# An attention and feed-forward kernel: the early batches' leftover scores beside the second visit, and one output block a half later

## The chip, the cores and the metric

The kernel runs on one core of a Trainium2 chip. The metric is the device time of one execution in microseconds. Kernel before: median 320.42 us of 13 runs (319.06 to 323.31).

## What is computed

Attention with a relative position bias over 8 batches, 8 heads, 576 positions and 64 dimensions per head, then a feed-forward layer that takes the largest of three products. In short:

```
scores = q @ k.T / 8 + bias_table[bucket(|i - j|)]     # per batch and head, 576 x 576
attn   = softmax(scores) @ v
x      = attn, heads side by side                       # 4608 tokens x 512
h      = max(x @ w1, x @ w2, x @ w3)                    # 4608 x 768
out    = h @ w_out                                      # 4608 x 512, float32
```

The bucket depends on the distance alone and is constant beyond a limit, so the bias is applied as a factor after the exponential, in a band near the diagonal only; elsewhere it is a constant that cancels in the softmax.

## The kernel before

**Tiles.** 576 positions are four tiles of 128 and a leftover of 64. Heads go in pairs (hp 0 to 3). A pair's exponentials lie in e4 (four key tiles, two heads, 512 queries) and in el, which takes the leftovers: first the leftover 64 keys of both heads against all 576 queries ("left keys", score tile sct, lines 573 to 581), then the leftover 64 queries against the four key tiles ("left queries", score tile scq, 547 to 551 and 589 to 594).

**The loop over pairs** (813 to 894; batches 1 to 7, four pairs each; batch 0 has loops of its own ahead of it). A pair is worked in two halves, each of which begins with a visit (554 to 571): for 256 queries, two score tiles sc of eight matmuls in all, each with a 1024-wide exponential on ScalarE. Between the visits stand the attention products of the pair before (attend, 604 to 652), the leftover scores, the band multiplications on VectorE (times_band, 529 to 536), and matmuls of the feed-forward layer of tokens that are done.

**attend** is kept back in a list, late, two entries for a pair: half 0 has 18 matmuls, half 1 has 27, since it also takes the leftover queries. Each accumulates in one bank of ps_a. Its quotients (638 to 651) are a reciprocal and a multiplication on VectorE; for the last pair of a batch they also issue transposing DMAs on SyncE's queue that put the result in xT, which the feed-forward layer reads.

**PSUM.** Three pools with two buffers each, handed out in turn: ps_s (two banks each: sc, sct, scq of left_queries, and tp, the transposes of batch 1's queries and keys), ps_a (one bank: attention sums, and scq in the new way), ps_f (one bank: feed-forward products, outputs, the x transposes).

**Two ways for a pair.** In line 818, together is true for batches 3 to 7 and for (2, 1) to (2, 3). There the left queries are scored in the second visit, ahead of its sc tiles, in two ps_a banks, with two 256-wide exponentials (556 to 559); both attention halves of the pair before run in the first half, the second one right after the left keys (844 to 847); and the second half's fill runs with idle_sums set, so that the feed-forward layer's first products use ps_a (339). For batch 1 and (2, 0), attention half 1 follows the second visit (860 to 863), and the left queries are scored inside the second fill, in a ps_s buffer, with one 512-wide exponential (880 to 881).

**Order.** All matmuls and transposes (93 to 97), VectorE's operations and most DMA issues are kept in program order; the exponentials and some ScalarE copies are not pinned. In batch 1, second_transposes (507 to 527, called in line 865) stands behind the second visit; it makes the next pair's qT and kT by ten transposes into one ps_s buffer and copies on VectorE and ScalarE.

**The fill** (439 to 451). The feed-forward layer is cut in portions with a weight that counts 128x512 matmuls (two 128x256 ones count as one). fill(rate, hooks) takes portions, at least one, until the next would pass the rate, and calls its hooks just before the last groups of these. Rate is 8 in batch 1 and (2, 0), else 13 (819). The portions that fall to the pairs concerned, in units of a 128x512 matmul, first half + second half: (1, 0) and (1, 1) 4 + 8, (1, 2), (1, 3) and (2, 0) 8 + 4, (2, 1) 12 + 6. The 12 are two output blocks of six matmuls (output, 362 to 393), the 6 a third one.

**Loads.** load_qk(3) in line 874 is gated by the quotients of attend(1, 3, 1); it is issued on GpSimd's queue. load_v(2) in line 871 stands ahead of it there.

Of the kernel before, what the change touches and what calls it, by code (L numbers as in the profile page):

```python
# [39 lines left out]
def kernel(  # L40
# [21 lines left out]
    QM = 2 * QS  # L62
# [28 lines left out]
    inorder = tc.keep_in_program_order  # L91

    def mm(*args, **kw):
        inorder(nc.tensor.matmul(*args, **kw))  # L94
# [322 lines left out]
    pending, rest, stores, deferred, idle_sums = [], [], [], [], []  # L417

    def store_outputs():

        while stores:
            stores.pop(0)()
# [7 lines left out]
    def early():  # L430

        if pending and None in pending[0][1]:
            n, fns = pending[0]
            i = fns.index(None)
            for fn in fns[:i]:
                fn()
            pending[0] = (n, fns[i + 1 :])

    def fill(target, *hooks):

        groups, spent, hooks = [], 0, list(hooks)
        while pending and (not groups or spent + pending[0][0] <= target):
            n, fns = pending.pop(0)
            spent += n
            groups += [fn for fn in fns if fn]
        for j, group in enumerate(groups):
            while hooks and (j == len(groups) - 1 or j > 0 and len(hooks) > len(groups) - 1 - j):
                hooks.pop(0)()
            group()
        for hook in hooks:  # L450
            hook()


    def transposes(b):

        made = qk_tiles()
        qk.append(made)

        def one(j, t):
            n = P if t < KT or j else S - KT * P  # L460
            src = batch[b][j][:, t].rearrange("p h d -> p (h d)") if t < KT else (
                (qtail, ktail)[j][b % 2][0:n].rearrange("p h c -> p (h c)")
            )
            turned_qk[b, j, t] = inorder(nc.sync.dma_start_transpose(out=made[j][:, :, P * t : P * t + n], in_=src))  # L464

        for t in range(KT + 1):
            one(0, t)
            one(1, t)
            yield
# [59 lines left out]
    def times_band(hp, e4, t, lo, hi, put=lambda x: x):  # L529
        lo, hi = max(lo, P * t - P), min(hi, P * t + 2 * P)  # L530
        if lo < hi:
            c0, c1 = BAND - (hi - P * t + P), BAND - (lo - P * t + P)
            put(nc.vector.tensor_tensor(  # L533
                out=e4[:, t, :, lo:hi], in0=e4[:, t, :, lo:hi],
                in1=hank[:, 2 * hp : 2 * hp + 2, c0:c1][:, :, ::-1], op=ALU.mult,
            ))

    def exp(out_, in_):
        nc.scalar.activation(out=out_, in_=in_, func=ACTF.Exp, scale=inv_sqrt_d)  # L539

    def put_left_queries(el, banks):

        eq = el[:, S:].rearrange("p (t h q) -> p t h q", t=KT, h=2)
        for par, bank in enumerate(banks):
            exp(eq[:, :, par, :], bank.rearrange("p (t q) -> p t q", t=KT))

    def turn_left_queries(qT, kT, banks):

        for t in range(KT):
            for par, bank in enumerate(banks):  # L550
                r = slice(64 * par, 64 * par + 64)
                mm(bank[:, 64 * t : 64 * t + 64], lhsT=kT[r, P * t : P * t + P], rhs=qT[r, QM:S])

    def visit(qT, kT, e4, c, mid=None, el=None):

        if el is not None:
            banks = [ps_a.tile([P, KT * 64], F32, tag="a", name="scq") for _ in range(2)]
            turn_left_queries(qT, kT, banks)
            put_left_queries(el, banks)
        for tt in range(0, KT, 2):  # L560
            sc = ps_s.tile([P, 2, 2, QS], F32, tag="sc", name="sc")
            for t in range(2):
                for par in range(2):
                    r = slice(64 * par, 64 * par + 64)
                    mm(
                        sc[:, par, t, :], lhsT=kT[r, P * (tt + t) : P * (tt + t) + P],
                        rhs=qT[r, c * QS : c * QS + QS],
                    )
            exp(e4[:, tt : tt + 2, :, c * QS : c * QS + QS].rearrange("p t h q -> p h t q"), sc[:])
            if tt == 0 and mid:  # L570
                mid()
# [17 lines left out]
    def left_queries(hp, qT, kT, el):  # L589

        sc = ps_s.tile([P, 2, CH], F32, tag="sc", name="scq")
        turn_left_queries(qT, kT, [sc[:, par, 0 : KT * 64] for par in range(2)])
        eq = el[:, S:].rearrange("p (t h q) -> p h t q", t=KT, h=2)
        exp(eq, sc[:, :, 0 : KT * 64].rearrange("p h (t q) -> p h t q", t=KT))
# [70 lines left out]
    def x_tile():  # L665
        return xs.tile([P, KT + 1, d_model], BF16, tag="x_sb", name="x_sb")
# [3 lines left out]
    def next_late():  # L670
        return late.pop(0)() if late else (lambda: None)

    def e_tiles():
        return (
            ep.tile([P, KT, 2, QM], BF16, tag="e4", name="e4"),
            ep.tile([P, S + KT * P], BF16, tag="el", name="el"),
        )
# [49 lines left out]
    for hp in range(HP):  # L727
        qT, kT = (x[:, hp, :] for x in qk[0])
        e4, el = e_tiles()
# [28 lines left out]
    for hp in range(HP):  # L758
        qT, kT = (x[:, hp, :] for x in qk[0])
        e4, el = e_tiles()  # L760
# [11 lines left out]
        def keys():  # L772
            left_keys(hp, qT, kT, el, QS, S)
# [7 lines left out]
        quotients = next_late()  # L781
# [5 lines left out]
        if hp < 2:  # L787
# [5 lines left out]
            quotients = next_late()  # L793
# [19 lines left out]
    for b, hp in [(b, hp) for b in range(1, B) for hp in range(HP)]:  # L813
        if hp == 0:
            x_sb[b] = x_tile()
        qT, kT = (x[:, hp, :] for x in qk[b])
        e4, el = e_tiles()
        together = b > 1 and (b, hp) != (2, 0)
        rate = 8 if b == 1 or (b, hp) == (2, 0) else 13

        visit(qT, kT, e4, 0)
        store_outputs()
        if b == 1:
            if hp == 0:
                crossbar = transposes(2)
            next(crossbar, None)
        elif hp and b + 1 < B:
            if hp == 1:  # L830
                crossbar = transposes(b + 1)
            next(crossbar)
        early()
        if turned:
            turned.pop(0)()
        quotients = next_late()
        times_band(hp, e4, 0, 0, QS, inorder)
        quotients()
        if b == 1 and hp + 1 < HP:
            spread_packed(hp + 1, nc.vector)  # L840
        if (b, hp) == (1, 1):
            add_ffn(QS, QS)

        def keys():
            left_keys(hp, qT, kT, el, 0, S)
            if together:
                next_late()()

        fill(rate, keys, *([lambda: None] if together else []))
        times_bandt(hp, el)  # L850


        visit(qT, kT, e4, 1, el=el if together else None)
        store_outputs()
        if b == 1 or hp in (1, 2) and b + 1 < B:
            next(crossbar, None)
        early()
        if turned:
            turned.pop(0)()
        if not together:  # L860
            quotients = next_late()
            times_band(hp, e4, 1, 0, QM, inorder)
            quotients()
        if b == 1 and hp + 1 < HP:
            second_transposes(qk[1], hp + 1)
        if hp == 1 and b > 1:
            add_ffn((b - 1) * CH, CH)
        if hp == (2, 2, 0)[min(b, 3) - 1] and b + 1 < B:
            if b == 1:
                load_last_weights(turned_qk[2, 1, 1])  # L870
            load_v(b + 1, 0, H, turned_qk[b + 1, 1, KT - 1] if b < 3 else None)
        if (b, hp) == (2, 0):
            batch[3] = load_tiles()
            load_qk(3, divided[1, HP - 1, 1])
        if hp == 2 and 1 < b < B - 2:
            batch[b + 2] = load_tiles()
            load_qk(b + 2, turned_qk[b + 1, 1, KT - 1])

        def queries():
            if not together:  # L880
                left_queries(hp, qT, kT, el)
            times_band(hp, e4, 3, 0, QM, inorder)

        def bands_2():
            for t in range(1 if together else 2, 3):
                times_band(hp, e4, t, 0, QM, inorder)

        if together:
            idle_sums.append(hp)
        fill(rate, bands_2, queries)  # L890
        idle_sums.clear()
        times_band_left(hp, el)
        for half in range(2):
            late.append(lambda b=b, hp=hp, e4=e4, el=el, half=half: attend(b, hp, e4, el, half))
# [44 lines left out]
```

## Time and profile before

| | |
|---|---|
| median of 13 runs | 320.42 us |
| the profiled execution: time, span | 321.07 us, 319.3 us |
| TensorE busy | 306.3 us (96%) |
| VectorE busy | 213.4 us (67%) |
| ScalarE busy | 201.1 us (63%) |
| GpSimd busy | 108.3 us (34%) |
| 1024-wide exponential (sc) | 128 of 1030 ns |
| 576-wide exponential (sct) | 28 of 655 ns |
| 512-wide exponential (scq, old way) | 9 of 598 ns |
| 256-wide exponential (scq, new way) | 46 of 381 ns |
| granted TensorE clock | full, but for 18.2 to 25.0 us of the span, where it is half |

How to read the profile: times are microseconds unless marked ns; a row gives the source line, the engine, the operation, output and input by the program's names, the shape and the count. PE is TensorE's matmuls, PEld its weight loads, DVE VectorE, ACT ScalarE, POOL GpSimd, SP SyncE. Matmuls overlap in the pipeline, so what a group of them costs is read from the start of one group to the start of the next and not from their lengths. Line 94 is the helper that issues every matmul, so the groups are told apart by their tiles.

### The profile page before, as it was taken

The numbers are of one execution on the slowest core, as the hardware profiler recorded it, in microseconds if no ns is written. First come the engines' busy times: TensorE is split into PE (matmuls) and PEld (weight loads), VectorE is DVE, ScalarE is ACT, GpSimd is POOL, SyncE is SP. The second block draws the span as 40 slices with busy tenths as digits, with TensorE's granted clock in tenths as the row PEclk, the third lists the DMA queues.
The fourth block names the chain that finished last, engine by engine and source line by source line (L and its number), as shares of the span: only waits on it lengthen the run. The fifth ranks groups of instructions, "written<-read, shape, count | busy, mean of one in ns | idle before, by whom it ended". The sixth has DMA issues, their size and how long they took to land.

```text
span 319.3 us, 8238 instructions
## 1 busy us (share of the span) xinstructions
PE 306.3 (96%) x3328; PEld 172.0 (54%) x3328; DVE 213.4 (67%) x535; ACT 201.1 (63%) x297; POOL 108.3 (34%) x143
## 2 busy tenths in 40 slices
PE   7768999999999999999999999999999999999995
PEld 2346777775555555555555555555555555444442
DVE  6387778786667766666677767777667675554552
ACT  4958998896777667766777677667776751121221
POOL 8938741348049530952087019600000000000000
PEclk9969999999999999999999999999999999999999
DMA  9999999999999999999999999994042103301103
GB/s 165 192 198 199 182 144 134 142 109 140 193 152 151 130 199 163 85 131 196 175 83 146 161 204 119 154 223 95 2 77 99 36 2 74 133 0 71 62 0 131
DMA packets 163878, 40.34 MB, mean 126 GB/s; under 512 B 153720, under 2 KB 159360, under 8 KB 163840
## 3 DMA queue, kind: packets, MB, share of 16 engines
q0 software_dynamic: 103776, 16.66, 79.1%
q1 hardware_dynamic: 58304, 22.69, 39.6%
q10 hardware_dynamic: 1760, 0.47, 0.7%
q8 instruction: 26, 0.43, 0.6%
q14 instruction: 12, 0.10, 0.1%
HBM read 35.39 MB, written 9.45 MB: 140 GB/s over the span
## 4 chain that ended last, share of the span: by engine, by line
PE 70%; DMA 3%; SPq 2%; ACT 1%; DVE 0%; issue 0%; DVEq 0%
PE ps L94 37%; PE pso L94 13%; PE a L94 11%; PE sc L94 6%; DMA kT<-ktail 2%; SPq L464 2%; PE sct L94 2%; PE scq L94 1%; DMA out_dram<-osb 1%; ACT e L539 0%; DVE m L354 0%; ACT osb L388 0%; ACT osb L107 0%; SPq L389 0%; DVE el L585 0%
## 5 line engine op out<-in xcount | busy, mean ns | idle before, releaser
L94 PE MATMUL ps<-xT,w_bf 128*128 128x512 bf16 (+1 forms) x720 | 152.2, 358 | 0.0
L539 ACT ACTIVATE e<-sc 128x1024 bf16<-128x1024 f32 x128 | 124.3, 1030 | 20.5 <-PE sc L94 18.1
L94 PEld LDWEIGHTS <-w_bf 128*128 128x128 bf16 x720 | 65.3, 98 | 62.7 <-issue 5.0
L533 DVE TENSOR_TENSOR e<-e,hank 128x512 bf16<-128x512 bf16 (+2 forms) x136 | 59.0, 469 | 12.0 <-ACT e L539 9.9
L345 ACT ACTIVATE m<-ps 128x512 bf16<-128x512 f32 x48 | 29.2, 608 | 51.9 <-PE ps L94 51.9
L354 DVE TENSOR_TENSOR m<-ps,m 128x512 bf16<-128x512 f32 x48 | 33.1, 689 | 34.2 <-PE ps L94 34.0
L94 PE MATMUL pso<-wo_bf,hT 128*128 128x512 bf16 (+2 forms) x222 | 50.3, 373 | 0.0
L94 PEld LDWEIGHTS <-kT 64*128 64x128 bf16 (+1 forms) x832 | 29.8, 95 | 37.2 <-issue 24.0
L94 PE MATMUL a<-vx,e 128*128 128x65 bf16 x1024 | 46.4, 195 | 0.0
L94 PE MATMUL sc<-qT,kT 64*128 64x256 bf16 x512 | 41.0, 273 | 2.9 <-ACT e L539 1.3
L360 DVE TENSOR_TENSOR hT<-ps,m 128x512 bf16<-128x512 f32 x48 | 33.0, 688 | 15.9 <-PE ps L94 14.5
L94 PEld LDWEIGHTS <-e 128*128 128x128 bf16 x1024 | 42.1, 99 | 0.8
L139 POOL DMA_DIRECT2D vx<-in_v_dram x32 | 28.3, 905 | 30.2 <-DMA kT<-k_sb 13.5
L94 PE MATMUL a<-vt,el 128*128 128x130 bf16 x160 | 36.0, 225 | 1.2 <-DMA vt<-in_v_dram 1.2
L167 POOL DMA_DIRECT2D q_sb<-in_q_dram x24 | 22.0, 918 | 43.9 <-DMA kT<-k_sb 12.9
L110 DVE COPY osb<-pso 128x512 f32<-128x512 f32 (+1 forms) x33 | 22.6, 686 | 18.0 <-PE pso L94 14.7
L641 DVE TENSOR_TENSOR x_sb<-a,rd 128x256 bf16<-128x256 f32 (+1 forms) x64 | 31.4, 491 | 2.2
L539 ACT ACTIVATE el<-scq 128x256 bf16<-128x256 f32 (+1 forms) x55 | 20.5, 416 | 19.5 <-PE scq L94 19.4
L94 PEld LDWEIGHTS <-hT 128*128 128x128 bf16 x222 | 20.1, 97 | 22.4 <-issue 1.5
L94 PEld LDWEIGHTS <-el 128*128 128x128 bf16 x416 | 24.3, 97 | 10.4 <-issue 5.5
L539 ACT ACTIVATE el<-sct 128x576 bf16<-128x576 f32 (+2 forms) x36 | 21.7, 606 | 6.6 <-PE sct L94 5.3
L167 POOL DMA_DIRECT2D k_sb<-in_k_dram x24 | 22.1, 919 | 1.2 <-DMA w_bf<-in_moe_w_dram 1.2
(71 smaller groups left out, 168.2 us busy)
## 6 DMA issues: line engine op xcount, KB each, us to landing
out_dram<-osb SPq DMA_DIRECT2D x35, 256.0 KB, 3.1
vx<-in_v_dram POOLq DMA_DIRECT2D x32, 128.0 KB, 8.3
q_sb<-in_q_dram POOLq DMA_DIRECT2D x26, 128.0 KB, 6.0
k_sb<-in_k_dram POOLq DMA_DIRECT2D x24, 128.0 KB, 6.8
w_bf<-in_moe_w_dram POOLq DMA_DIRECT2D x3, 768.0 KB, 10.5
xT<-in_k_dram SPq DMA_DIRECT2D x6, 128.0 KB, 4.5
hank<-w_dr SPq DMA_DIRECT2D x2, 384.0 KB, 6.4
wo_bf<-in_moe_w_out_dram POOLq DMA_DIRECT2D x1, 768.0 KB, 8.3
```

The source lines that it names most:

```text
L94: inorder(nc.tensor.matmul(*args, **kw))
L110: return inorder(nc.vector.tensor_copy(out_, in_))
L139: in_turn(b, nc.gpsimd.dma_start(out=dst[:, t, h0:h1, :], in_=x[:, t, h0:h1, :])) for t in range(t0, t1)
L167: loads.append(in_turn(b, nc.gpsimd.dma_start(out=dst[:, t], in_=main_part(src, b)[:, t])))
L345: nc.scalar.activation(out=st[fb]["m0"][:], in_=ps0, func=ACTF.Copy)
L354: inorder(nc.vector.tensor_tensor(out=m[:], in0=ps1, in1=st[fb]["m0"][:], op=ALU.max))
L360: inorder(nc.vector.tensor_tensor(out=block(fb), in0=ps2, in1=other, op=ALU.max))
L464: turned_qk[b, j, t] = inorder(nc.sync.dma_start_transpose(out=made[j][:, :, P * t : P * t + n], in_=src))
L533: put(nc.vector.tensor_tensor(out=e4[:, t, :, lo:hi], in0=e4[:, t, :, lo:hi], in1=hank[:, 2 * hp : 2 * hp + 2, c0:c1][:, :, ::-1], op=ALU. ...
L539: nc.scalar.activation(out=out_, in_=in_, func=ACTF.Exp, scale=inv_sqrt_d)
L641: divided[b, hp, half] = inorder(nc.vector.tensor_tensor(out=x_sb[b][:, 2 * half : 2 * half + n, P * hp : P * hp + P].rearrange("p t (h d) ...
```

## The change

All pairs from batch 1 on are done the one way. For batch 1 and (2, 0) this means: attention half 1 of the pair before moves from behind the second visit into the first fill, right after the left keys; the left queries move from the second fill into the second visit, ahead of its score tiles, from one ps_s buffer to two ps_a banks, with two exponentials instead of one; band 1 moves into the second fill; idle_sums is set there. The second hook of the first fill does nothing and moves the left keys a group ahead where there are three groups or more. In (2, 1) the first fill gets rate 8 instead of 13, so that one of its two output blocks goes to the second half.

```diff
-        together = b > 1 and (b, hp) != (2, 0)
         rate = 8 if b == 1 or (b, hp) == (2, 0) else 13
...
         def keys():
             left_keys(hp, qT, kT, el, 0, S)
-            if together:
-                next_late()()
-
-        fill(rate, keys, *([lambda: None] if together else []))
+            next_late()()
+
+        fill(8 if (b, hp) == (2, 1) else rate, keys, lambda: None)
         times_bandt(hp, el)
...
-        visit(qT, kT, e4, 1, el=el if together else None)
+        visit(qT, kT, e4, 1, el=el)
...
-        if not together:
-            quotients = next_late()
-            times_band(hp, e4, 1, 0, QM, inorder)
-            quotients()
...
         def queries():
-            if not together:
-                left_queries(hp, qT, kT, el)
             times_band(hp, e4, 3, 0, QM, inorder)
...
         def bands_2():
-            for t in range(1 if together else 2, 3):
+            for t in range(1, 3):
                 times_band(hp, e4, t, 0, QM, inorder)
...
-        if together:
-            idle_sums.append(hp)
+        idle_sums.append(hp)
         fill(rate, bands_2, queries)
```

## The prediction, before the result was known

> **What bounds the kernel now.** I read first the engine shares of the page. TensorE is busy for 96% of the 319.3 us span, VectorE 67%, ScalarE 63%, so time is won or lost where TensorE stands still or does a step in a slow form. I call a run of the loop for one batch and one pair of heads a pair and write it (b, pair), as in the code, counted from 0. The change touches (1, 0) to (2, 1), so the second view is the table of windows, cut where each pair's first score matmul starts. The columns after the window are its length and the busy time of TensorE, weight loads, VectorE, ScalarE and GpSimd, then the clock.
>
> ```profile
> 43.21:50.52 7.31, 7.05 (x110) 5.30 (x110) 6.00 (x17) 6.02 (x9) 1.92 (x3) 1.00 2.58 115
> 50.52:57.38 6.86, 6.66 (x106) 5.25 (x106) 5.42 (x17) 6.06 (x9) 0.84 (x1) 1.00 1.36 153
> 57.38:63.42 6.04, 6.04 (x96) 4.67 (x96) 4.42 (x13) 5.33 (x7) 2.69 (x4) 1.00 1.18 149
> 63.42:69.46 6.04, 6.04 (x96) 4.66 (x96) 4.55 (x13) 5.41 (x8) 2.06 (x3) 1.00 1.57 127
> 76.51:85.86 9.35, 8.94 (x99) 4.74 (x99) 6.76 (x17) 6.81 (x10) 2.15 (x4) 1.00 1.82 175
> 85.86:94.19 8.33, 8.33 (x96) 4.53 (x95) 5.88 (x16) 6.17 (x9) 2.01 (x3) 1.00 0.99 178
> ```
>
> These are (1, 1), (1, 2), (1, 3), (2, 0), (2, 2), (2, 3). In the last, a normal late pair, ScalarE works 6.17 of 8.33 us. In the first four it works 5.3 to 6.1 of 6.0 to 7.3: TensorE leads ScalarE by little there, because such a pair has half the feed-forward work. The third view is the timeline of TensorE (start, length, what, idle time before it).
>
> ```profile
> 45.98 0.39 PE L94 MATMUL sc<-qT,kT 64*128 64x256 bf16 x4
> 46.55 0.39 PE L94 MATMUL sc<-qT,kT 64*128 64x256 bf16 x4 [0.18 <-ACT el L539]
> ...
> 51.67 1.04 PE L94 MATMUL ps<-xT,w_bf 128*128 128x256 bf16 x8
> 52.54 0.41 PE L94 MATMUL sct<-qT,kT 128*128 128x512 bf16 x2
> 52.78 1.04 PE L94 MATMUL ps<-xT,w_bf 128*128 128x256 bf16 x8
> 53.76 0.66 PE L94 MATMUL sc<-qT,kT 64*128 64x256 bf16 x8
> ...
> 56.18 0.29 PE L94 MATMUL scq<-qT,kT 64*128 64x64 bf16 x8 [0.20 <-ACT e L539]
> 56.40 1.05 PE L94 MATMUL ps<-xT,w_bf 128*128 128x256 bf16 x8
> 57.38 0.61 PE L94 MATMUL sc<-qT,kT 64*128 64x256 bf16 x8
> ```
>
> Two things are to be seen. The second score tile waits at 46.55 for the exponential two tiles back: ps_s hands its two buffers out in turn. And the same eight ps matmuls take 0.87 us from start to start ahead of a 128-row matmul (51.67 to 52.54), but 0.98 ahead of a 64-row one (52.78 to 53.76).
>
> The pair (2, 1) is done the new way already, with a short second half, and shows what follows the new order:
>
> ```profile
> 74.44 0.29 PE L94 MATMUL scq<-qT,kT 64*128 64x64 bf16 x8
> 74.57 0.60 PE L94 MATMUL sc<-qT,kT 64*128 64x256 bf16 x8
> 75.11 1.47 PE L94 MATMUL pso<-wo_bf,hT 128*128 128x512 bf16 x6
> 76.51 0.39 PE L94 MATMUL sc<-qT,kT 64*128 64x256 bf16 x4
> 77.31 0.39 PE L94 MATMUL sc<-qT,kT 64*128 64x256 bf16 x4 [0.41 <-ACT e L539]
> ```
>
> ScalarE's timeline beside it:
>
> ```profile
> 74.77 0.66 ACT L539 ACTIVATE el<-scq 128x256 bf16<-128x256 f32 x2 [1.76 <-PE scq L94]
> 75.31 3.78 ACT L539 ACTIVATE e<-sc 128x1024 bf16<-128x1024 f32 x4
> ```
>
> From the start of scq, call it t0, the two 256-wide exponentials begin at +0.33, the first wide one at +0.87, and four wide ones take 3.78, so they follow at (3.78 - 1.03)/3 = 0.917. The first ends at +1.90, the second at +2.82. TensorE used the second's buffer at +2.87, so a buffer is free 0.05 after its exponential. **The two releases, t0 + 1.95 and t0 + 2.87**, price the change.
>
> **What the Trainium skill says.** "TensorEngine Tiling (Array Packing)", Key Properties: a change of tiling mode drains the engine. The 0.87 against 0.98 agrees: about 0.11 for a change from 128 to 64 rows. "ScalarE: Activation LUTs", What ACT_TABLE_LOAD costs: an instruction with immediate scale and bias takes 186 ns + 0.833 per element, and neighbours overlap by 93 ns. The rows have 381 ns (256 wide), 598 (512) and 1030 (1024), where it gives 399, 613 and 1039. "TensorE: Matmul & The Clock Gate", Part 2, Step-by-step: matmuls stay in program order, only weight loads are pulled ahead. So a matmul that waits for a bank holds all behind it; the trace agrees at 77.31, where the attention follows the late score tile.
>
> **The change part by part**, for TensorE.
>
> Leftover scores beside the second visit. The eight scq took 0.23 (56.18 to 56.40) between 128-row work and take 0.13 (74.44 to 74.57) ahead of sc. With the drain before them (0.11), about 0.20 is saved in each of five pairs. The tile also leaves ps_s. On ScalarE one exponential of 598 ns becomes two of 381: 0.54 start to start instead of 0.51, nothing by itself. But they now stand ahead of the second visit's exponentials, which end 0.3 later than without.
>
> Attention half 1 into the first half. The same 27 matmuls (0.91 us) and two VectorE instructions; nothing saved or added in sum. It **takes cover away**. Now it lies between the second visit's scores and the transposes of the next pair's queries and keys (tp, also in ps_s): for (1, 1) 46.88 to 47.79. After the change tp follows the scores at t0 + 0.13 + 0.54 = 0.67, and its buffer is that of the first score tile, free at 1.95. Stall 1.28 in (1, 1) and (1, 2); in (1, 0) the transposes x_transposes (0.18, in ps_f) lie between, so 1.1. Queued behind tp are this half's feed-forward matmuls and the next visit.
>
> (1, 3) and (2, 0) have no tp. Scores to 0.67, one feed-forward group of 0.98 to 1.65; the next visit's second tile could start at 1.92, and starts at 2.87: 0.95 lost each. VectorE's bands need the same exponentials and end before the attention tile that reads them.
>
> Ring stalls that go: (1, 0) 0.31 (39.08 - 38.50 - 0.27), (1, 1) 0.30 (46.55 - 45.98 - 0.27), both for the sct exponential, which half 1's 0.91 us now covers; (1, 2) 0.27 at 56.18.
>
> Bank wait that comes: scq takes both ps_a banks, so its second matmul waits for half 1's quotients. From the last attention matmul's start to their end is 1.03 in (1, 0) before (40.45 to 41.48), against a cover of 0.97 (one group); in (1, 0) VectorE is also busy with the copies of spread_packed. No run shows this wait. Below it is zero; above, with VectorE a feed-forward maximum late (0.69), about 0.6 per pair. I take 0.15 for (1, 0), 0.05 for (1, 1), none after.
>
> One output block later. (2, 1) goes from 12 + 6 to 6 + 12 matmuls. The second half then covers: t0 + 0.67 + 2.7 is past 2.87, and the stall at 77.31 (77.31 - 76.51 - 0.27 = 0.53) goes. I take 0.59 with the drain in it. In the first half 1.38 us still cover the quotients' 1.03. Its PSUM copy (0.69) and its store move with it.
>
> What else moves: quotients of (1, 3) half 1 come half a pair earlier, and with them three transposing DMAs on SP and the gate of load_qk(3), eleven loads on GpSimd's queue. GpSimd's v loads stand ahead till 65.5, SP's transposes run to 74.25, and xT is first read at 80.68: free, over 6 us of cover. If it went, TensorE would wait for the last transpose, 1.6 us. Band 1's move to the fill and f2 in a ps_a bank in (1, 0) cost nothing: VectorE is idle behind the transposes, and the bank's exponential ended 1.5 us before. If that cover failed, an exponential's 0.4.
>
> **The sum** against the profiled execution (321.07, span 319.3, 1.77 around it):
> - (1, 0): 1.1 + 0.15 - 0.31 - 0.20 = +0.7
> - (1, 1): 1.28 + 0.05 - 0.30 - 0.20 = +0.8
> - (1, 2): 1.28 - 0.27 - 0.20 = +0.8
> - (1, 3) and (2, 0): 0.95 - 0.20 = +0.75 each
> - (2, 1): -0.6
>
> Together +3.2: 324.3 against 321.07. From (2, 3) on TensorE has no idle time, so nothing gives it back. The runs' median is 320.42, so I forecast 320.42 + 3.2 = 323.6.
>
> **The rivals.**
> - **Bank waits**: quotients late by about 0.4 in four pairs, +1.6: 325.2. For it: VectorE works 5.4 to 6.0 us of these pairs. Against: its queue is short when half 1 ends. Chance 0.14.
> - **Exponentials reordered**: ScalarE's are not pinned to program order. With the wide ones first they start 0.43 after their scores (as at 53.76, 54.19) and release at 0.13 + 0.43 + 1.03 + 0.05 = 1.64, 0.3 earlier in five pairs: 323.6 - 1.5 = 322.1. Against: program order at 74.77 and 82.83. 0.08.
> - **Clock drop**: the clock fell to half for 6.8 us (18.2 to 25.0) after 3.4 us with 1.57 of TensorE work. The new stalls leave about 2.1 in 3.4, and after 2.20 (25.0 to 28.4) it held. One drop costs 3.4: 327.0. 0.05.
> - **Buffers free earlier, so faster**: if the score buffers came free s earlier than my two releases, each of five stalls shrinks by s. Even at 3.2/5 = 0.64; faster by the bound from 0.84 on; at s = 1.0 it is 320.42 + 3.2 - 5 x 0.97 = 318.8. The savings (1.0 of drains, 0.9 of ring stalls, 0.6 in (2, 1)) would then stand alone. Against: one exponential lasts 1.03, and no order above gives over 0.3. 0.07.
> - **No difference** (s from 0.6 to 0.84, or the new order idle in part): 320.4. 0.06.
>
> **Chances.** The forecast has 0.60. A measurement of this kernel tells about 0.3% (1 us) from no change. Slower: 0.60 + 0.14 + 0.08 + 0.05 = 0.87; within: 0.06; faster: 0.07. The range goes from 321.8, below the reordered case, to 325.6, above the bank waits; outside lie the clock drop and the last two, 0.18.
>
> **What would show it.** Right: tp waits over 1 us for ACT e in three pairs; two late second tiles at t0 + 2.87; scq in 0.13; no stall at the start of (2, 2). Wrong: tp straight after the scores, or t0 pushed late by VectorE. Pairs of about 8.1 us for (1, 1), 7.7 for (1, 2) and 6.8 for (1, 3) are the check.

## The result and the profile after

The kernel after takes 323.73 us (median of 11 runs, 323.12 to 325.75) against 320.54 us (48 runs): 1.0107 times as long, 95% interval 1.009 to 1.0125. The forecast was 323.6 us, slower. The profiled execution took 324.02 us with a span of 322.2; before it was 321.07 with 319.3, so 2.95 us more.

The table of windows of the kernel after, cut where each pair's first score matmul starts; the rows are (1, 1), (1, 2), (1, 3), (2, 0) and (2, 2), the columns those of the prediction, with the DMA engines' share and GB/s at the end:

```profile
43.75:51.82 8.07, 6.79 (x110) 5.50 (x110) 5.64 (x17) 5.96 (x10) 1.04 (x2) 1.00 2.27 131
51.82:59.48 7.66, 6.46 (x107) 5.25 (x107) 5.55 (x17) 6.12 (x10) 1.24 (x2) 1.00 0.95 139
59.48:65.67 6.19, 5.97 (x96) 4.77 (x96) 4.49 (x14) 4.59 (x8) 4.35 (x6) 1.00 1.92 150
65.67:72.53 6.86, 6.11 (x96) 4.74 (x95) 4.65 (x13) 5.47 (x9) 1.69 (x2) 1.00 0.57 57
80.28:89.04 8.76, 8.76 (x98) 4.73 (x98) 6.36 (x16) 6.17 (x9) 0.00 (x0) 1.00 1.69 161
```

TensorE's busy time within (1, 1) fell from 7.05 to 6.79 us while the pair grew from 7.31 to 8.07: the added time is time in which TensorE stands still. The timeline of TensorE names it, line by line:

```profile
46.45 1.03 PE L94 MATMUL ps<-xT,w_bf 128*128 128x256 bf16 x8
47.42 0.36 PE L94 MATMUL scq<-qT,kT 64*128 64x64 bf16 x8
47.59 0.62 PE L94 MATMUL sc<-qT,kT 64*128 64x256 bf16 x8
49.42 0.38 PE L97 MATMUL tp<-ident,q_sb 128*128 128x128 bf16 x4 [1.21 <-ACT e L539]
...
65.67 0.39 PE L94 MATMUL sc<-qT,kT 64*128 64x256 bf16 x4 [0.23 <-ACT e L539]
66.59 0.39 PE L94 MATMUL sc<-qT,kT 64*128 64x256 bf16 x4 [0.52 <-ACT e L539]
...
77.58 2.76 PE L94 MATMUL pso<-wo_bf,hT 128*128 128x512 bf16 x12
80.28 0.61 PE L94 MATMUL sc<-qT,kT 64*128 64x256 bf16 x8
```

And ScalarE's beside it:

```profile
47.79 0.66 ACT L539 ACTIVATE el<-scq 128x256 bf16<-128x256 f32 x2 [0.75 <-PE scq L94]
48.34 1.95 ACT L539 ACTIVATE e<-sc 128x1024 bf16<-128x1024 f32 x2
```

In (1, 1) scq starts at t0 = 47.42, the wide exponentials at t0 + 0.92, and the transposes tp at t0 + 2.00, straight behind the first of these: the forecast release was t0 + 1.95. In (1, 3), with t0 = 63.67, the next visit's second tile starts at 66.59 = t0 + 2.92 (forecast 2.87). The stall at the start of (2, 2) is gone: two output blocks, 12 matmuls, then all eight score matmuls without a break.

Added up from the start of one pair's attention half 0 to the next (or, for the first three, from score matmul to score matmul):

| pair | forecast | measured |
|---|---|---|
| (1, 0) | +0.7 | 8.25 - 7.59 = +0.66 |
| (1, 1) | +0.8 | 8.07 - 7.31 = +0.76 |
| (1, 2) | +0.8 | 7.66 - 6.86 = +0.80 |
| (1, 3) | +0.75 | 6.90 - 6.04 = +0.86 |
| (2, 0) | +0.75 | 6.85 - 6.03 = +0.82 |
| (2, 1) | -0.6 | 7.05 - 7.64 = -0.59 |
| sum | +3.2 | +3.3 |

The span grew by 2.9 only. Of the difference of 0.4, 0.12 lies ahead of (1, 0), and 0.23 in the pair (3, 3), far behind the change: from the left queries of one pair to those of the next it takes 8.56 us before (124.18 to 132.74) and 8.33 after (127.36 to 135.69). The forecast missed this second part: a wait of the kernel before that the kernel after did not meet (its line stands below, under "Nothing gives it back").

### The profile page after: what moved, and what is told of

Read it like the earlier page. It is cut to its first block, busy times and chain, and to the rows that moved or that the text cites. A ratio compares the mean times of both kernels' runs of the same rounds, so it can differ in the third digit from the quotient of the medians.

```text
span 322.2 us, 8244 instructions
## 1 busy us (share of the span) xinstructions
PE 307.7 (95%) x3328; PEld 172.9 (54%) x3328; DVE 212.8 (66%) x535; ACT 201.4 (62%) x302; POOL 108.1 (34%) x143
## 4 chain that ended last, share of the span: by engine, by line
PE 75%; DMA 1%; ACT 1%; issue 0%
PE ps L94 39%; PE pso L94 14%; PE a L94 12%; PE sc L94 7%; PE sct L94 2%; PE scq L94 2%; DMA out_dram<-osb 1%; ACT e L539 0%; ACT osb L388 0%; ACT osb L107 0%
## 5 line engine op out<-in xcount | busy, mean ns | idle before, releaser
L533 DVE TENSOR_TENSOR e<-e,hank 128x512 bf16<-128x512 bf16 (+2 forms) x136 | 58.2, 466 | 9.0 <-ACT e L539 8.5
L94 PE MATMUL sc<-qT,kT 64*128 64x256 bf16 x512 | 41.8, 278 | 3.3 <-ACT e L539 2.3
```

The lines of the kernel that those rows point to most:

```text
L533: put(nc.vector.tensor_tensor(out=e4[:, t, :, lo:hi], in0=e4[:, t, :, lo:hi], in1=hank[:, 2 * hp : 2 * hp + 2, c0:c1][:, :, ::-1], op=ALU. ...
```

## The experiments

Theory: half 1 of the attention was the cover for the second visit's exponentials. Moved away, it leaves TensorE waiting for the first of them (three pairs, at the transposes) or the second (two pairs, at the next visit). Rival: the left queries beside the visit are what costs, by their two exponentials and their two sum banks. A second rival: ScalarE's load sets the pace of these pairs, and the waits only show where.

One measure serves for all traces: the time from the left queries of (0, 3) to those of (2, 2), which holds all the changed pairs and neither the start of the kernel nor (3, 3). The waits named are from each run's own timeline of TensorE. A ratio is against the runs of the kernel before that were taken along with that kernel. Each trace is one execution, and not always a typical one: the traces of the late output block alone (322.45 us) and of the left queries beside only (324.38) are the longest of their 14 runs.

| kernel | median us | ratio to before (95%) | (0, 3) to (2, 2) |
|---|---|---|---|
| before | 320.5 | 1 | 49.00 |
| after | 323.73 | 1.0107 (1.009 to 1.0125) | 52.31 |
| late output block only | 320.19 | 0.9999 (0.9975 to 1.0023) | 49.11 |
| half 1 early only | 323.89 | 1.0109 (1.0077 to 1.0141) | 52.34 |
| left queries beside only | 319.68 | 0.9988 (0.9955 to 1.002) | see below |
| after, half 1 late in (1, 0) to (1, 2) | 321.23 | 1.0004 (0.9984 to 1.0024) | 49.87 |
| after, half 1 late in (1, 3), (2, 0) | 322.73 | 1.0054 (1.0032 to 1.0075) | 51.10 |
| after, transposes behind a group | 323.06 | 1.0089 (1.0068 to 1.011) | 51.69 |
| after, transposes in ps_f | 322.57 | 1.007 (1.0041 to 1.0099) | 51.30 |
| after, v early | 323.35 | 1.0096 (1.0077 to 1.0115) | 52.60 |
| before, v early | 320.5 | 1.0005 (0.9987 to 1.0023) | 49.00 |
| mixed, v early | 320.65 | 1.0008 (0.9986 to 1.003) | 48.22 |
| mixed, v, q and k early | 320.13 | 0.9986 (0.996 to 1.0012) | 48.65 |
| before, v, q and k early | 319.81 | 0.9979 (0.9962 to 0.9995) | 49.00 |

### Half 1 early, the left queries as before

```diff
 # kernel after, where apart = b == 1 or (b, hp) == (2, 0)
-        visit(qT, kT, e4, 1, el=el)
+        visit(qT, kT, e4, 1, el=None if apart else el)
...
         def queries():
+            if apart:
+                left_queries(hp, qT, kT, el)
             times_band(hp, e4, 3, 0, QM, inorder)
```

> Kernel after, but in batch 1 and (2, 0) the left queries stay in the second fill in a ps_s buffer with one 512-wide exponential, as before; attention half 1 stays in the first half, the late output block too. My theory, that the loss is the cover taken away behind the second visit: the transposes wait about 0.95 us for the first score tile's exponential in three pairs (0.8 in the first), scq waits about as long for the same buffer in (1, 3) and (2, 0): +3.5 against before, about 324.0, slower than before as the whole change is. Rival, that the loss comes from the left queries beside the visit (two exponentials ahead of the visit's own, both sum banks taken): without them about 319.5 to 320.

323.89 us, and 52.34 us in the measure: the whole loss, without the left queries beside the visit. The timeline of TensorE shows the wait at the transposes of (1, 2) and, in (1, 3), at scq, which here is in ps_s and has the same buffer:

```profile
56.93 0.38 PE L97 MATMUL tp<-ident,q_sb 128*128 128x128 bf16 x4 [0.90 <-ACT e L539]
...
64.69 0.29 PE L94 MATMUL scq<-qT,kT 64*128 64x64 bf16 x8 [0.90 <-ACT e L539]
```

The first rival is out: the loss is as large without it. The wait is 0.9 (0.95 expected) and not 1.2, since no narrow exponentials stand ahead, but scq takes its 0.23 us between 128-row matmuls again (64.69 to 64.92).

### The left queries beside the visit, half 1 as before

```diff
 # kernel after, same apart
-            next_late()()
+            if not apart:
+                next_late()()
...
+        if apart:
+            quotients = next_late()
+            times_band(hp, e4, 1, 0, QM, inorder)
+            quotients()
...
-            for t in range(1, 3):
+            for t in range(2 if apart else 1, 3):
```

> Kernel after, but in batch 1 and (2, 0) attention half 1 stays behind the second visit with band 1, as before; the left queries are beside the second visit and the output block is late, as after. My theory: half 1's 0.91 us cover the first exponential, so the transposes wait only about 0.37 us in (1, 1) and (1, 2) and 0.2 in (1, 0), the drains around scq (0.2 in five pairs) and most of the ring stalls are saved: 1.0 + 0.3 + 0.3 + 0.6 - 0.95 = 1.2 less than before, about 319.3. Rival, that the left queries beside the visit are what costs: slower than before, 322 or more.

319.68 us: the loss is gone, and the expected gain (319.3) is not clear of the noise. The intervals from (1, 0) to the start of (2, 1) sum to 33.47 us (34.30 to 67.77), 0.37 less than before (35.62 to 69.46). Then this happened in the profiled execution, the longest of the 14, by TensorE's timeline:

```profile
71.39 0.29 PE L94 MATMUL a<-vt,el 128*128 128x130 bf16 x1 [2.97 <-DMA vt<-in_v_dram]
```

The attention of batch 2 waited 2.97 us for v, and the clock was at half until 77 us; with both, the measure is 53.84. The runs reach from 318.59 to 324.38. That opened a new question: does something stop a faster batch 1?

### The late output block alone

```diff
 # kernel before
-        fill(rate, keys, *([lambda: None] if together else []))
+        fill(8 if (b, hp) == (2, 1) else rate, keys, *([lambda: None] if together else []))
```

> Kernel before with one edit: the first fill of (2, 1) gets rate 8, so that one output block goes to the second half. My theory: the stall of 0.53 us at the second score tile of (2, 2) goes and nothing else changes: about 0.6 us less than before, 319.9. Rival, that the block only moves a wait from one half to the other: no change, 320.5, and another matmul in (2, 1) waits for 0.5 us.

A miss: 320.19, ratio 0.9999. The stall at (2, 2) is gone, as in the kernel after. The trace, of an execution 2.3 us above the median, shows two other waits:

```profile
70.85 0.22 PE L94 MATMUL a<-vt,el 128*128 128x130 bf16 x1 [0.65 <-DMA vt<-in_v_dram]
...
128.73 0.28 PE L94 MATMUL sc<-qT,kT 64*128 64x256 bf16 x2 [0.46 <-DMA kT<-k_sb]
131.15 0.42 PE L94 MATMUL sct<-qT,kT 128*128 128x512 bf16 x2 [0.56 <-DMA kT<-ktail]
```

The first is ahead of the edit's own effect and differs from one execution to the next: v lands about when it is needed. It hides what the rival had foreseen, another wait in (2, 1): with one output block in the first half, the left keys stand ahead of that block, and their buffer comes free with an exponential that ends at 71.10 here. Had v been in time, they would have waited some 0.4 us for it (an estimate: scores at 69.59, then 0.54 and 0.61 of matmuls, release at 71.15). The next section shows that wait where nothing hides it. By this estimate the late block alone is worth about 0.2 us and not 0.6, less than these runs can tell from nothing.

The second is in the pair (3, 3), whose interval is 9.71 us here, 8.56 before, and 8.33 where nothing waits. Here the transposed leftover keys of batch 4 (ktail), issued at 123.20, let TensorE start at 131.15 only.

### Which pairs lose how much

The edit of "left queries beside only", with apart narrowed to the three pairs that have transposes behind the visit, and to the two that don't:

```diff
+        apart = b == 1 and hp < HP - 1          # first three
+        apart = (b, hp) in ((1, 3), (2, 0))     # last two, a kernel of its own
```

> Kernel after, but in (1, 0) to (1, 2), the three pairs with transposes, attention half 1 is behind the second visit again (the left queries stay beside the visit). My theory: the transposes wait 0.3 us and not 1.2 for the first exponential: by the pair times of the run with the left queries beside only, 0.9 + 0.85 + 0.6 = 2.3 less than after, 321.4. With the run on the other two pairs it adds up to the whole loss: 1.8 + 2.3 = 4.1, less what a load takes back at 130 us. Rival as there: no change, 323.7.

> Kernel after, but in (1, 3) and (2, 0), the two pairs without transposes, attention half 1 is behind the second visit again (the left queries stay beside the visit). My theory: half 1's 0.91 us covers the second exponential, the late second tiles at the start of (2, 0) and (2, 1) go, 0.9 each: 1.8 less than after, 321.9. Rival, that ScalarE's load and not the order sets the pace of these two pairs: no change, 323.7.

Half 1 behind the visit in the first three pairs gives 2.44 us back in the measure (52.31 - 49.87; expected 2.3), in the last two 1.21 (expected 1.8; the median of 322.73, for 321.9, is a miss). In (1, 1) of the first kernel the transposes no longer show a wait:

```profile
45.38 0.84 PE L94 MATMUL sc<-qT,kT 64*128 64x256 bf16 x8
...
47.30 0.38 PE L97 MATMUL tp<-ident,q_sb 128*128 128x128 bf16 x4
```

The last two pairs themselves did what was expected of them: from attention half 0 in (1, 3) to that in (2, 1) it takes 11.92 us (59.21 to 71.13) where the kernel after has 13.75, 1.83 less. Two waits outside took the rest back. The bank wait of (1, 0), which this kernel shares with the kernel after, was 0.25 longer in this execution. The other is in (2, 1), by the timelines of TensorE and of ScalarE:

```profile
71.50 0.50 PE L94 MATMUL a<-vx,e 128*128 128x65 bf16 x8
72.12 0.41 PE L94 MATMUL sct<-qT,kT 128*128 128x512 bf16 x2
```

```profile
71.04 1.94 ACT L539 ACTIVATE e<-sc 128x1024 bf16<-128x1024 f32 x2 [0.29 <-ACT e L539]
```

The attention is through at 71.74 (eight of its narrow matmuls take 0.24 from start to start), but the left keys start at 72.12, 0.05 behind the end of the first exponential (71.04 + 1.03): 0.38 lost. The output block that covered this exponential in the kernel before has gone to the second half. In the kernel after nothing waits there, because the second score tile is late itself. The mixed kernel below shows the same wait, and there the late block brought 0.2.

The account closes: the five pairs lost 3.90 (the table above without (2, 1)), and with half 1 late in all five they are 0.37 shorter than before, 4.27 in all. Undone apart, they gave 2.36 (the first three, from first score matmul to first score matmul) and 1.83, together 4.19. ScalarE's work is the same in all three kernels (201.4, 200.9 and 201.5 us busy), so the second rival is out as well: the order makes the waits.

### The same instructions, the transposes covered

```diff
 # kernel after
-        if b == 1 and hp + 1 < HP:
-            second_transposes(qk[1], hp + 1)
+        turn = [lambda: second_transposes(qk[1], hp + 1)] if b == 1 and hp + 1 < HP else []
...
-        fill(rate, bands_2, queries)
+        fill(rate, *turn, bands_2, queries)
```

> Kernel after with one edit: in batch 1 the transposes of the next pair stand behind the first feed-forward group of the second half where it has two ((1, 0) and (1, 1)), ahead of the only one in (1, 2). The same instructions, only their order on TensorE differs. My theory, that the loss is missing cover: 0.87 us of matmuls hide most of the wait, which falls from 1.1 to about 0.25 in (1, 0) and from 1.2 to about 0.4 in (1, 1): 1.7 less than after, about 322.0. Rival, that ScalarE's load or another wait would take its place: no change, 323.7.

In (1, 1) the theory holds: the wait fell from 1.21 to 0.23, and the interval that holds it from 8.53 to 7.71. In (1, 0) it doesn't. TensorE's timeline has the visit behind (1, 0), then the transposes of (1, 1):

```profile
42.80 0.61 PE L94 MATMUL sc<-qT,kT 64*128 64x256 bf16 x8 [0.64 <-ACT kT L107]
...
48.48 0.38 PE L97 MATMUL tp<-ident,q_sb 128*128 128x128 bf16 x4 [0.23 <-ACT e L539]
```

In (1, 0) the feed-forward group ahead has a ScalarE copy of its own, which now stands ahead of the copies that make kT, so the next visit waits for kT. With a longer bank wait (scq to sc 0.62 us, 0.25 in the kernel after) this pair lost 0.2. 323.06 us, 0.7 less than after instead of 1.7.

```diff
 # kernel after, in second_transposes, for the transposes of (1, 1) to (1, 3)
+            for j, (tl, n) in enumerate(((qtail, S), (ktail, (KT + 1) * P))):
+                tp = ps_f.tile([P, 2 * CH], BF16, tag="ff", name="tp")
...
+                dve_copy(made[j][:, hp, KT * P :], tp[:, KT * P : n])
```

> Kernel after with one edit: the transposes of (1, 1) to (1, 3)'s queries and keys go to two ps_f banks instead of one ps_s buffer, and VectorE makes all four copies. My theory: the wait of the transposes for the first exponential (about 1.2 us in three pairs) goes; part of it comes back as waits of the feed-forward products for these ps_f banks, since VectorE's four copies take 1.6 us, and of the next visit for the keys. I work out t0 + 3.3, 3.9 and 3.05 for the start of the next visit where the kernel after has 4.5, 4.4 and 3.5: 2.1 less than after, about 321.6. Rival, that those 1.2 us are only where a wait shows and ScalarE's load would stop TensorE elsewhere: no change, 323.7.

322.57 us, 1.2 less instead of 2.1. (1, 1) and (1, 2) gave 0.5 each, as worked out; in (1, 0) nothing was won: x_transposes still held one ps_f bank (its copy runs on ScalarE at 42.29, behind the exponentials), so the key transposes waited 0.89 for the bank of the query transposes, whose copy on VectorE ended at 41.74. The expected 1.2 there was wrong, since that buffer was left out of the count.

### Does a late load cap a faster batch 1?

```diff
-            load_v(b + 1, 0, H, turned_qk[b + 1, 1, KT - 1] if b < 3 else None)
+            load_v(b + 1, 0, H, (turned_qk[2, 1, 2] if b == 1 else turned_qk[b + 1, 1, KT - 1]) if b < 3 else None)
```

> Kernel before with one edit: the loads of batch 2's v go behind the third key transpose of batch 2 instead of the fourth, so GpSimd issues them some 2 to 3 us earlier. Theory, from the run with the late output block alone: these loads land at about 70 us, just when attention (2, 0) half 0 needs them, in some executions later, and cap what a faster batch 1 can bring. Then the slow tail of the executions shrinks and the median falls by up to 0.5 us (320.0 to 320.5). Rival, that the earlier loads slow the transposes that (2, 0) needs: slower by 1 us or more.

> Kernel after with one edit: batch 2's v loads early, as in the other run. My theory: nothing in the kernel after waits for v, since its batch 1 is 3.9 us longer: no change, 323.7. Rival, that part of the loss is a late load: up to 1 us less.

No change to the kernel before (ratio 1.0005). The kernel after gave 323.35, 0.4 less than its own median of 323.73, and the two intervals overlap. Neither in its trace (measure 52.60) nor in that of the kernel after does TensorE wait for v, so no part of the loss is shown to be a late load. "Mixed" is the kernel with the left queries beside the visit except in (1, 2), half 1 late, the output block late and v early:

```diff
 # left queries beside only, with v early
+        beside = (b, hp) != (1, 2)
-        visit(qT, kT, e4, 1, el=el)
+        visit(qT, kT, e4, 1, el=el if beside else None)
...
         def queries():
+            if not beside:
+                left_queries(hp, qT, kT, el)
             times_band(hp, e4, 3, 0, QM, inorder)
```

> Left queries beside the second visit in batch 1 and (2, 0) except (1, 2), attention half 1 behind the second visit as before, the late output block, and the v loads of batch 2 early. My theory, from the trace of the run with the left queries beside only: (1, 0) -0.27, (1, 1) -0.09, (1, 3) -0.17, (2, 0) -0.05, the late block -0.55 once v has landed in time: 1.1 less than before, about 319.4. Rival, that the v loads' arrival still sets when (2, 1) starts its attention: 320.3.

320.65, though in its trace the measure is 0.78 us shorter than before (48.22): (3, 3) took 9.81 us there, waiting for the keys of batch 4, and gave it all back. Earlier loads for batch 3, ahead in that chain:

```diff
-            load_qk(3, divided[1, HP - 1, 1])
+            load_qk(3, divided[1, HP - 1, 0])
```

> The mixed kernel (left queries beside the visit but in (1, 2), half 1 behind it, late output block, v of batch 2 early) with one more edit: the q and k loads of batch 3 go behind the quotients of half 0 of (1, 3) instead of half 1. Theory, from that kernel's trace: its gain of 1.5 us is taken back at 127 to 130 us, where (4, 0) waits for the DMA transposes of batch 4's keys, the end of a chain of loads and transposes that starts with these loads. Starting it some 3 us earlier gives the gain back: 319.5 and a lower upper end. Rival, that the chain's pace is the DMA engines' and not its start: no change, 320.6.

> Kernel before with the two early loads alone (v of batch 2; q and k of batch 3). Theory: the kernel before loses 0.2 us in the pair (3, 3) to the same chain, so there is little to win: 320.2. Rival, that the chain is what slows the kernel before in its longer executions: 319.7 or less. If the earlier loads disturb the transposes of x, slower.

With them, (3, 3) takes 8.34 and 8.33. The mixed kernel then loses 0.43 at 80 us to the transposes of x (its measure goes from 48.22 to 48.65) and ends at 320.13, its interval including no change. The kernel before with the two edited loads is at 319.81, ratio 0.9979 (0.9962 to 0.9995), with its changed pairs as before (49.00). That is some 0.7 us, where the theory had 0.2 and the rival 0.8 or more, and the trace doesn't explain it: its span is 319.3, as before.

How far the chain of loads sets the pace stays open. In the mixed kernel the last transpose of the keys was issued at 121.6 with both loads early, at 122.7 without, and the wait is gone, as the theory has it. But in the kernel before it was issued at 122.87, and with the two loads edited no earlier, at 123.16, where nothing waited for it. And it was issued at 123.20 with the late output block alone and at 123.19 with half 1 late in the first three pairs: in the first TensorE waited until 131.15, in the second the keys were there by 129.97. So the time from issue to landing differs by over a microsecond between executions; no run here shows why. A wait in (3, 3) can take a gain back, as in two of these traces. That it caps every faster batch 1 is not shown.

## Why the prediction was right, point by point

- **The two releases.** t0 + 1.95 and t0 + 2.87 were forecast from the pair (2, 1) of the kernel before; the pairs show 2.00 and 2.92. The 0.05 is the second bank's wait, which delays the exponentials. This step carried the forecast, and its terms, left unrounded, sum to 3.28 against the 3.31 of the pairs.
- **Cover taken away.** From where the transposes could have started to where they did it takes 49.42 - 47.59 - 0.54 = 1.29 us in (1, 1), as much in (1, 2), and 41.35 - 40.08 - 0.18 = 1.09 in (1, 0); the forecast was 1.28 and 1.1. Undone in these pairs alone, 2.4 of the 3.3 us come back.
- **Late second tiles.** 66.59 - 65.67 = 0.92 from first to second tile, instead of 0.27, and 0.23 of idle ahead of the first. The forecast did not name the first tile's wait; the second's hides it. The pairs grew by 0.86 and 0.82, forecast 0.75.
- **Drains and ring stalls.** In the kernel after they fit: for (1, 1), 1.29 + 0.04 of bank wait - 0.30 - 0.20 = 0.83 against 0.76 measured. By themselves they are worth less: with half 1 late (1, 0), (1, 1), (1, 3) and (2, 0) are 0.27, 0.09, 0.17 and 0.05 shorter than before and (1, 2) is 0.21 longer, since the next visit waits 0.30 for VectorE's copy of qT. The sum is 0.37, where the expectation of that run had 0.6 ahead of (2, 1).
- **The bank wait.** Forecast 0.15 in (1, 0) and 0.05 in (1, 1), none after. The eight scq take 0.25 in (1, 0) and 0.17 to 0.19 in the next four, against 0.13 undisturbed: 0.12, and 0.04 to 0.06 in each of four. VectorE's timeline gives the reason:

```profile
46.88 0.56 DVE L641 TENSOR_TENSOR x_sb<-a,rd 128x384 bf16<-128x384 f32 x1
```

  Its end, 47.44, is 0.02 behind the first scq. Sum 0.31 instead of 0.20. In other executions it was more: idle 0.20 and 0.32 in (1, 0) of two kernels with the same order.
- **The late output block.** -0.59 measured, -0.6 forecast, in the kernel after. The forecast was lucky here: it did not ask what the block had covered in the first half, and only because the second score tile comes late in the new order do the left keys not wait there. Without that, the block brings about 0.2.
- **"Nothing gives it back."** This sentence was wrong by 0.23 us. In (3, 3) of the kernel before a weight load waits for the keys of batch 4, and 0.2 us of that is not covered by matmuls. By the timeline of the weight loads:

```profile
129.76 0.11 PEld L94 LDWEIGHTS <-kT 128*128 128x128 bf16 x2 [0.54 <-DMA kT<-ktail]
```

  The page had the hint, in the chain that ended last; these are its shares by engine:

```profile
PE 70%; DMA 3%; SPq 2%; ACT 1%; DVE 0%; issue 0%; DVEq 0%
```

  and those of the kernel after:

```profile
PE 75%; DMA 1%; ACT 1%; issue 0%
```

  Before, the chain ran through DMA and SyncE's queue: (4, 0) came when the keys of batch 4 did. The kernel after comes 3 us later and did not meet that wait.
- **The number.** That 323.73 lies within 0.2 us of 323.6 is in part luck: the pairs lost 0.1 more than the rounded sum, 0.35 of the span's difference lies elsewhere, and the medians are 3.19 apart where the profiled executions are 2.95.

## What to carry to other kernels

Before moving work out from behind a matmul that waits for another engine, ask what it covered: take the release time from a place that already runs in the new order, and set it against the start of what comes next in the queue. Here several small savings per pair (drains of 0.2 us, ring stalls of 0.3) didn't pay for one lost cover of 0.9. The same question is due for work that is moved to remove a stall: the output block that filled a gap of 0.6 us in one half had covered 0.4 us in the other. And look in the chain that ended last for a share of DMA, however small: where one stands, there can be a wait behind the changed stage that takes up part of a shift ahead of it.

## What was not expected of the hardware

In the one execution with the 2.97 us wait for v, the TensorE clock fell to half 1.9 us after the last matmul (68.41 to 70.3) and stayed so for 6.8 us (0.50 in each full microsecond from 71 to 77). The waits of 0.93 to 1.21 us in the kernel after, some 8 us apart, left it at full speed (1.00 in every window above); around them TensorE still worked 2.2 of 3.4 us (2.21 from 46.0 to 49.4, 2.19 from 47.6 to 51.0), as the clock rival of the prediction had it. "TensorE: Matmul & The Clock Gate", Why this matters for your kernels, in the Trainium skill, asks for no gaps above some 3 us between bursts of matmuls. Here the clock fell 1.9 us into a gap, and in the kernel before it fell at 18.2 us, after 3.4 us with 1.57 us of work, with no wait over 0.80 us just ahead:

```profile
17.07 0.30 PE L94 MATMUL sct<-qT,kT 128*128 128x320 bf16 x1 [0.80 <-ACT e L539]
17.98 0.32 PE L94 MATMUL scq<-qT,kT 64*128 64x64 bf16 x8 [0.62 <-ACT e L539]
```

In these traces the length of one gap alone does not tell when the clock falls.
